# The router's transposes on VectorE in 32x32 blocks, with the blocks moved through DRAM

## The chip, the cores and the metric

The kernel runs on one core of one Trainium2 chip. The metric is the device time of one launch in microseconds (us), the median of the runs shown. Engines are called PE (TensorE), DVE (VectorE), ACT (ScalarE), POOL (GpSimd) and SP (SyncE, which here only issues DMAs).

## The reference

Three layers, in float32. First a two-way attention between 8x8 heads of 512 tokens (64 wide) and 32 states, which leaves 8 x 544 = 4352 tokens of 512 features. Then a gated layer on all of them, then a routed one:

```
x  = (silu(x @ w_gate) * (x @ w_val)) @ w_out          # 512 -> 1536 -> 512
do = x @ w_skip > 0                                     # tokens to compute
logits = x[do] @ w_route ; e = argmax(logits)           # 8 experts
out[do] = x + prob[e] * (relu(x @ w1[e]) @ w2[e])       # 512 -> 1024 -> 512
```

The change touches only how `x @ w_skip` and `x @ w_route` (nine scores a token) get their operand.

## The kernel before

The tokens go through the gated layer in nine blocks: eight blocks `b` of 512 attention tokens and a last block (`b == B`) of the 256 state tokens. A block takes 12 steps `f`, one for each 128 of the 1536 inner features. In a step PE runs `l1(b, f)` (gate and value: 24 matmuls with fp32 split into a high and a low half, all of them `L388`) and `l2` of the step before (12 matmuls, `L442` to `L444`). Between the two, ACT takes the tanh (`L395`), DVE makes `hv` (`L396`, `L399`), ACT casts the high half `hh` (`L407`), and POOL (in the last stretch DVE) subtracts the low half `hl` (`L408`). In the text a "step" is one such `(b, f)`. At the third and seventh step of a block `sw_two` also makes the next weights (`L171`, `L299`, `L300`), and the attention of the next block is spread over the same steps.

At a block's end `evac` copies four 128x512 results from PSUM into `x2` (two on ACT, `L457`, two on DVE, `L455`) and SP stores `x2` twice, to `out` and to `x2_dram` (`L463`). In the next block's steps the router works on it: `score_T` transposes each 128x512 quarter with four 128x128 PE transposes into one PSUM bank (`L479`) and DVE copies the bank into `x2T` (`L480`); `score_mm` multiplies `x2T` by the nine score columns `w9` (`L489`); ACT copies the result into a corner of `x2T` (`s9`, `L494`); `score_sum` transposes that back (`L500`, `L501`); `route_a` and `route_b` choose the expert and the slot, and POOL writes a record of each token into the table `tab` (`L565`, `L566`, `L575`). The token in partition `p` of quarter `j` is row `4p + j` of the block.

The table `sc_at` says at which steps these pieces stand in the program. From there a scheduler sets the order on each engine by its own estimate of times, and each engine runs its instructions in that order; SP too issues DMAs strictly in order, and a DMA that must wait for data holds up the ones behind it. Near the end of the eighth block `first_pick` and `first_load` choose one expert and SP loads its 4 MB of weights; the last block's scores are thus worked on beside the split of these weights (`L805`) and `first_xT` (`L824`), whose low halves go into the tile `fxl`. Two groups of `score_T` at the very end serve the last block itself. What follows after about 737 us (the experts) the change doesn't touch.

Of the kernel before, what the change touches and what calls it, by code (L numbers as in the profile page):

```python
# [7 lines left out]
F32 = mybir.dt.float32  # L8
F32R = mybir.dt.float32r
# [11 lines left out]
B, H, S, NS, D = 8, 8, 512, 32, 64  # L21
# [4 lines left out]
T = S + NS  # L26
# [6 lines left out]
SS = 32  # L33
# [18 lines left out]
def attention_then_two_moe_kernel(  # L52
# [13 lines left out]
    nc = tc.nc  # L66

    const = ctx.enter_context(tc.tile_pool(name="const", bufs=1, side="left"))
    dram = ctx.enter_context(tc.tile_pool(name="dram", bufs=1, space=bass.MemoryType.DRAM))
# [20 lines left out]
    with ExitStack() as ph:  # L90
        left = ph.enter_context(ExitStack())
        wts = left.enter_context(tc.tile_pool(name="wts", bufs=1, side="left"))
        ahl = left.enter_context(tc.tile_pool(name="ahl", bufs=2, side="left"))
# [13 lines left out]
        def side_bank():  # L107
            return ps_q.tile([128, 512], F32, name=ROLE[2], tag=ROLE[2])
# [5 lines left out]
        w9 = wts.tile([128, 4, SS], F32, name="w9")  # L114
# [235 lines left out]
        HT, HV = {}, {}  # L350
# [97 lines left out]
        def evac(b, half):  # L448
# [21 lines left out]
                        nc.sync.dma_start(out=dst, in_=x2[:, t])  # L470
            HV[b] = (x2, sml.tile([128, 4, 9], F32, name="sc"))

        def score_T(b, t):
            x2, sc = HV[b]
            if t == 0:
                late["x2T"] = late["p"].tile([128, 4, 512], F32, name="x2T")
            p = side_bank()
            for j in range(4):
                nc.tensor.transpose(p[:, 128 * j:128 * j + 128], x2[:, t, 128 * j:128 * j + 128], ident)  # L479
            nc.vector.tensor_copy(  # L480
                late["x2T"][:, :, 128 * t:128 * t + 128], p.rearrange("p (j c) -> p j c", j=4)
            )

        def score_mm(b):
            nt = 4 if b < B else 2
            p = side_bank()
            for j in range(4):
                for t in range(nt):
                    nc.tensor.matmul(  # L489
                        p[SS * t:SS * t + SS, :128], w9[:, j], late["x2T"][:, j, 128 * t:128 * t + 128],  # L490
                        start=(j == 0), stop=(j == 3),
                    )
            late["s9"] = late["x2T"][:, 0, :128]
            nc.scalar.copy(late["s9"][:SS * nt], p[:SS * nt, :128])  # L494

        def score_sum(b):
# [48 lines left out]
        def route_b(b):  # L545
            nt, comp, ex, oh, ohb, cum, t8, t1, bc, be = RT.pop(b)
            p = side_bank()
            rk = p[:, :nt * E].rearrange("p (a b) -> p a b", b=E)
            nc.tensor.matmul(rk, tri, ohb, start=True, stop=False)
            nc.tensor.matmul(rk, ones, cum, start=False, stop=True)  # L550
            sl = t8("sl")
            nc.vector.tensor_tensor(out=sl, in0=rk, in1=be(ecap), op=ALU.add)
            nc.vector.tensor_tensor(out=sl, in0=sl, in1=oh, op=ALU.mult)
            s1 = t1("slot")
            nc.vector.tensor_reduce(out=s1, in_=sl, op=ALU.add, axis=AX.X)
            nc.vector.tensor_scalar(comp, comp, -BIG, BIG, op0=ALU.mult, op1=ALU.add)
            si = t1("si", I32)
            nc.vector.tensor_tensor(out=si, in0=s1, in1=comp, op=ALU.add)
            g = t1("g")
            nc.vector.tensor_reduce(out=g, in_=ex, op=ALU.add, axis=AX.X)  # L560
            nc.vector.tensor_scalar(g, g, 1e-9, None, op0=ALU.add)
            rec = sml.tile([128, 4, 3], I32, name="rec")
            nc.vector.reciprocal(rec.bitcast(F32)[:, :nt, 1], g)
            if b < B:
                nc.gpsimd.iota(rec[:, :, 0], [[1, 4]], base=b * T, channel_multiplier=4)  # L565
                nc.gpsimd.iota(rec[:, :, 2], [[1, 4]], base=b * S, channel_multiplier=4)  # L566
            else:
                for q in range(4):
                    nc.gpsimd.iota(
                        rec[32 * q:32 * q + 32, :nt, 0], [[4 * T, nt]], base=q * T + S, channel_multiplier=1  # L570
                    )
                nc.gpsimd.iota(rec[:, :nt, 2], [[128, nt]], base=B * S, channel_multiplier=1)
            done = []
            for t in range(nt):
                d = nc.gpsimd.indirect_dma_start(  # L575
                    out=tab[:, :], out_offset=bass.IndirectOffsetOnAxis(ap=si[:, t:t + 1], axis=0),
                    in_=rec[:, t, :], in_offset=None, bounds_check=E * CAP - 1, oob_is_err=False,
                ).ins
                if not done:
                    after_tab(d)  # L580
                for o in done:
                    tc.declare_no_dep(d, o, reason="each token has a row of its own")
                done.append(d)
            TAB[:] = done
# [228 lines left out]
        def first_xT():  # L813
            B0["xh"] = [
                wts.tile([128, 2, 512], F32R, name="fxh", tag="srT"), ahl.tile([128, 2, 512], F32R, name="ah")
            ]
            B0["xl"] = [
                late["p"].tile([128, 2, 512], F32R, name="fxl"), ahl.tile([128, 2, 512], F32R, name="al")
            ]
            for t in range(NT1):  # L820
                p = pair_bank() if t == 2 else ps_x.tile([128, 512], F32, name=f"px{2 + t}")
                s = slice(128 * t, 128 * t + 128)
                for k in range(K1):
                    nc.tensor.transpose(p[:, 128 * k:128 * k + 128], B0["xr"][t][:, 128 * k:128 * k + 128], ident)  # L824
                for a in range(2):
                    split(
                        B0["xh"][a][:, :, s], B0["xl"][a][:, :, s],
                        p[:, 256 * a:256 * a + 256].rearrange("p (k c) -> p k c", k=2),
                    )
# [76 lines left out]
        with tc.manual_schedule(engines={getattr(mybir.EngineType, e) for e in ("Activation", "DVE", "Pool")}):  # L906
# [99 lines left out]

        steps = [(b, f) for b in range(B + 1) for f in range(NF)]
        sc_at = {
            False: ({3: 0, 4: 2, 5: 3}, {3: 1}, 7, 8, 9),
            True: ({1: 0, 2: 1, 3: 2, 4: 3}, {}, 5, 6, 8),  # L1010
        }
        for i, (b, f) in enumerate(steps):
            if i < HAND:
                continue
            if i > HAND:
                l1(b, f)
            nb, nf = steps[min(i + 2, len(steps) - 1)]
            if nb < B:
                if nb == 0 and nf % 2 and i > HAND:
                    sw(nb, (nf - 1) // 2)  # L1020
            elif i + 2 < len(steps):
                sw_tok(nf, 0)
                sw_tok(nf, 1)
            sb, sc = att_at.get(i, ([], []))
            if b:
                mid, end, mm, sm, rt = sc_at[b == B]
                if f in mid:
                    sb = [lambda: score_T(b - 1, mid[f])] + sb
                if f in end:
                    sc = sc + [lambda: score_T(b - 1, end[f])]  # L1030
                if f == mm:
                    sb = sb + [lambda: score_mm(b - 1)]
                if f == sm:
                    sb = sb + [lambda: score_sum(b - 1), lambda: route_a(b - 1)]
                if f == rt:
                    sb = sb + [lambda: route_b(b - 1)]
            if 0 < b < B and f in (2, 6):
                sb = [lambda: sw_two(b, f // 2 + 1)] + sb
            if b < B - 1 and f == 10:
                sb = [lambda: sw_two(b + 1, 0)] + sb  # L1040
            conv_step(1 if b == 0 and i > HAND else 0)
            wo_split(b, f)
            if b == 0:
                if i == HAND:
                    sb = [lambda: a_srT(0)] + sb
                if f == 7:
                    load_w9()
                if f == 4:
                    init_tab()
            if b == B - 1 and f == 10:  # L1050
                sr_split()
            if b == B - 1 and f == 11:
                first_pick()
                first_load()
            if b == B and f == 10:
                first_xT()
            pb, pf = steps[i - 1]
            l2(pb, pf, 0)
            if pf == NF - 1:
                if pb == 0:  # L1060
                    open_late()
                evac(pb, 0)
            for t in sb:
                t()
            conv_step(f % 2 if b == 0 else 0)
            l2(pb, pf, 1)
            if pf == NF - 1:
                evac(pb, 1)
            for t in sc:
                t()  # L1070
            for _ in range((f > 3) + 2 * (f > 9) if b == B else 0):
                todo.pop(0)(pin=tc.keep_in_program_order)
            if f == 8 and b + 2 < B:
                load_T(b + 2)
                load_x(b + 2)
# [492 lines left out]
```

## Time and profile before

| | |
|---|---|
| median of 3 runs | 1012.24 us (1008.66 to 1014.16) |
| profiled execution | 1007.3 us, span 1005.6 us, mean granted PE clock 0.977 |
| PE busy | 957.1 us (95%), 6502 matmuls |
| DVE busy | 567.7 us (56%) |
| ACT busy | 438.1 us (44%) |
| POOL busy | 419.1 us (42%) |
| DMA | 103.18 MB, mean 103 GB/s over the span |

The span runs from the first to the last instruction; the time adds what lies around it. Busy shares are averages over stages that have different limits, so the prediction reads the stage in which the changed instructions stand. PE's rows overlap, since matmuls are pipelined: the distance between two starts is what a matmul costs, not its own duration.

### The profile page before, as it was taken

The page shows a single profiled execution, that of the slowest core. Times are in us where ns is not written, and L with a number is a line of the kernel's source. Part 1 is how long each engine was busy: PE and PEld are TensorE (multiplying, and loading weights), DVE is VectorE, ACT ScalarE, POOL GpSimd, SP SyncE. Part 2 cuts the span into 40 slices and gives each one's busy share as a digit, 9 for nine tenths or more (in the row PEclk, how much of TensorE's full clock was granted, in tenths as well). Part 3 has the DMA queues.
Part 4 walks back from the last instruction along what each step waited for, and adds up shares of the span by engine and source line. Part 5 has one row for each costly group of instructions (what it writes and reads, how often), then busy time and mean ns, then how long its engine had stood idle before and what let it go on. Part 6 is the DMA issues. An engine that isn't in the chain of part 4 may idle for free. (4 is left out here: it accounts for less than half of the span.)

```text
span 1005.6 us, 16950 instructions
## 1 busy us (share of the span) xinstructions
PE 957.1 (95%) x6502; PEld 730.6 (73%) x6502; DVE 567.7 (56%) x1155; ACT 438.1 (44%) x792; POOL 419.1 (42%) x413
## 2 busy tenths in 40 slices
PE   3999999999999999999999999999998888989897
PEld 2555777777777777777777777789887666767786
DVE  6989565564564565556555544678763542552361
ACT  5876443444444354354353343446513441443240
POOL 2001343653553554544454353320246545645711
PEclk7999999999999999999999999999999899989899
DMA  9891401111031030130020020051126538634441
GB/s 357 295 331 47 165 5 46 73 54 46 6 121 45 1 126 7 41 126 3 2 84 1 2 84 1 1 207 78 29 78 226 175 133 270 212 99 157 159 160 53
DMA packets 38762, 103.18 MB, mean 103 GB/s; under 512 B 14661, under 2 KB 15949, under 8 KB 34696
## 3 DMA queue, kind: packets, MB, share of 16 engines
q1 hardware_dynamic: 27080, 88.06, 24.2%
q0 software_dynamic: 11584, 13.87, 4.4%
q8 instruction: 54, 0.88, 0.4%
q14 instruction: 44, 0.36, 0.1%
HBM read 99.93 MB, written 23.24 MB: 122 GB/s over the span
## 5 line engine op out<-in xcount | busy, mean ns | idle before, releaser
L408 POOL TENSOR_TENSOR hl<-hv,hh 128x512 fp32r<-128x512 f32 x82 | 106.4, 1298 | 191.7 <-ACT hh L407 191.7
L442 PE MATMUL px<-wh,hh 128*128 128x512 f32 x376 | 154.6, 411 | 0.2 <-ACT hh L407 0.2
L388 PE MATMUL q<-ah,sh 128*128 128x512 f32 (+1 forms) x368 | 139.9, 380 | 8.9 <-ACT ah L247 8.0
L443 PE MATMUL px<-wl,hh 128*128 128x512 f32 x376 | 148.0, 394 | 0.0
L444 PE MATMUL px<-wh,hl 128*128 128x512 f32 x376 | 147.9, 393 | 0.0
L421 POOL TENSOR_TENSOR wl<-wo,wh 128x512 fp32r<-128x512 f32 x82 | 105.9, 1292 | 94.2 <-ACT wh L420 94.1
L388 PE MATMUL q<-ah,sl 128*128 128x512 f32 (+1 forms) x368 | 135.8, 369 | 0.1
L388 PE MATMUL q<-al,sh 128*128 128x512 f32 (+1 forms) x368 | 134.8, 367 | 0.0
L396 DVE SCALAR_TENSOR_TENSOR t<-t,q 128x512 f32<-128x512 f32 (+1 forms) x100 | 65.3, 653 | 115.5 <-ACT t L395 115.1
L407 ACT CAST hh<-hv 128x512 fp32r<-128x512 f32 (+1 forms) x100 | 59.5, 595 | 130.3 <-DVE hv L399 129.6
L420 ACT CAST wh<-wo 128x512 fp32r<-128x512 f32 x100 | 61.9, 619 | 81.5 <-PE px L444 72.2
L442 PEld LDWEIGHTS px<-wh,hh 128*128 128x128 f32 x376 | 70.6, 188 | 34.3 <-issue 20.0
L388 PEld LDWEIGHTS q<-ah,sh 128*128 128x128 f32 x368 | 69.8, 190 | 29.6 <-ACT ah L247 8.5
L444 PEld LDWEIGHTS px<-wh,hl 128*128 128x128 f32 x376 | 70.6, 188 | 16.3 <-DVE hl L408 0.2
L395 ACT ACTIVATE t<-q 128x512 f32<-128x512 f32 (+1 forms) x100 | 57.1, 571 | 57.0 <-PE q L388 56.0
L443 PEld LDWEIGHTS px<-wl,hh 128*128 128x128 f32 x376 | 70.8, 188 | 12.8
L388 PEld LDWEIGHTS q<-ah,sl 128*128 128x128 f32 x368 | 69.8, 190 | 13.2 <-DVE sl L342 0.5
L388 PEld LDWEIGHTS q<-al,sh 128*128 128x128 f32 x368 | 69.7, 190 | 12.6 <-issue 1.0
L388 PE MATMUL q<-ah,fh 128*128 128x512 f32 x224 | 76.3, 401 | 0.0
L1316 DVE SCALAR_TENSOR_TENSOR hl<-p,hh 128x512 fp32r<-128x512 f32 x28 | 19.4, 691 | 94.8 <-ACT hh L1315 69.2
L399 DVE SCALAR_TENSOR_TENSOR hv<-t,q 128x512 f32<-128x512 f32 (+1 forms) x100 | 65.5, 655 | 11.0
L804 ACT CAST kwsb<-r 128x512 fp32r<-128x512 f32 x120 | 67.7, 625 | 6.3 <-PE p L1331 3.0
(292 smaller groups left out, 1911.7 us busy)
## 6 DMA issues: line engine op xcount, KB each, us to landing
s1w<-in_moe_w_dram SPq DMA_DIRECT2D x14, 1024.0 KB
s2w<-in_moe_w_dram SPq DMA_DIRECT2D x14, 1024.0 KB
raw<-in_w_in_dram SPq DMA_DIRECT2D x12, 1023.8 KB
xt<-in_x_dram SPq DMA_DIRECT2D x8, 1024.0 KB
out_dram<-x SPq DMA_DIRECT2D x8, 1024.0 KB
x_dram<-x SPq DMA_DIRECT2D x8, 1024.0 KB
xT<-in_xT_dram SPq DMA_DIRECT2D x7, 1024.0 KB
raw<-in_w_out_dram SPq DMA_DIRECT2D x6, 1023.8 KB
```

Source lines behind the costliest of these rows:

```text
L388: nc.tensor.matmul(p[:, :n], w, m, start=start, stop=stop)
L395: nc.scalar.activation(t[:, :n], pg[:, :n], AF.Tanh, scale=0.5)
L396: nc.vector.scalar_tensor_tensor(out=t[:, :n], in0=t[:, :n], scalar=1.0, in1=pg[:, :n], op0=ALU.add, op1=ALU.mult)
L399: nc.vector.scalar_tensor_tensor(out=hv[:, :n], in0=t[:, :n], scalar=0.5, in1=pv[:, :n], op0=ALU.mult, op1=ALU.mult)
L407: nc.scalar.copy(hh[:, :n], hv[:, :n])
L408: low_eng(b, f).tensor_tensor(out=hl[:, :n], in0=hv[:, :n], in1=hh[:, :n].bitcast(F32), op=ALU.subtract)
L420: pin(nc.scalar.copy(wh, w))
L421: pin(low_eng(b, f).tensor_tensor(out=wl, in0=w, in1=wh.bitcast(F32), op=ALU.subtract))
L442: nc.tensor.matmul(p, hh[:, s], wh, start=(f == 0), stop=False)
L443: nc.tensor.matmul(p, hh[:, s], wl, start=False, stop=False)
L444: nc.tensor.matmul(p, hl[:, s], wh, start=False, stop=(f == NF - 1))
L804: pin(nc.scalar.copy(hi, src))
```

## The change

For the eight blocks of attention tokens `score_T` is replaced by `score_pair(b, h)`, which takes two quarters at once (`h` is 0 or 1). DVE transposes each quarter in 32x32 blocks into `x2b`; four DMAs, one from each 32 partitions, write the blocks into a DRAM scratch `swap` with the block rows and columns exchanged; one DMA reads it back as half of `x2T`, whose layout is new. `score_mm` reads its 128 columns from there in four runs of 32. Tokens come out in another order, so the record's row numbers are made by eight small `iota`s in place of two. The last block keeps `score_T`. `x2b` has one buffer and shares it with `fxl`; `swap` has two.

```
+        def score_pair(b, h):
+            x2 = HV[b][0]
+            if h == 0:
+                late["x2T"] = late["p"].tile([128, 2, 4, 2, 4, 32], F32, name="x2T", tag="x2T")
+            x2b = late["p"].tile([128, 4, 2, 128], F32, name="x2b", tag="fxl")
+            swap = dram.tile([4, 32, 4, 256], F32, name="swap", bufs=2)
+            for t in range(2):
+                nc.vector.transpose(
+                    x2b[:, :, t].rearrange("p g (k q) -> p k g q", k=4),
+                    x2[:, 2 * h + t].rearrange("p (k g q) -> p k g q", k=4, g=4),
+                )
+            for a in range(4):
+                nc.sync.dma_start(
+                    out=swap[:, :, a].rearrange("g q x -> q g x"),
+                    in_=x2b[32 * a:32 * a + 32].rearrange("q g t x -> q g (t x)"),
+                )
+            nc.sync.dma_start(
+                out=late["x2T"][:, h].rearrange("p a t k q -> p (a t k q)"), in_=swap.rearrange("g q a x -> (g q) (a x)")
+            )
...
+            if b < B:
+                nt, of = 4, lambda j, t: x2T[:, :, t, :, j]
...
-                        p[SS * t:SS * t + SS, :128], w9[:, j], late["x2T"][:, j, 128 * t:128 * t + 128],
-                        start=(j == 0), stop=(j == 3),
+                        p[SS * t:SS * t + SS, :128], w9[:, j], of(j, t), start=(j == 0), stop=(j == 3),
...
-                nc.gpsimd.iota(rec[:, :, 0], [[1, 4]], base=b * T, channel_multiplier=4)
-                nc.gpsimd.iota(rec[:, :, 2], [[1, 4]], base=b * S, channel_multiplier=4)
+                for t in range(4):
+                    for k, o in ((0, b * T), (2, b * S)):
+                        nc.gpsimd.iota(
+                            rec[32 * t:32 * t + 32, :, k], [[128, 4]], base=o + t, channel_multiplier=4
+                        )
...
         sc_at = {
-            False: ({3: 0, 4: 2, 5: 3}, {3: 1}, 7, 8, 9),
-            True: ({1: 0, 2: 1, 3: 2, 4: 3}, {}, 5, 6, 8),
+            False: ({1: 0, 4: 1}, 7, 8, 9),
+            True: ({1: 0, 3: 1}, 6, 7, 8),
         }
```

The scheduler places the new instructions. On SP, after the second block (`x_1870` is its `x2`), the order before was:

```order
L463 DMA out_dram<-x_1870 128x2048
L463 DMA x_dram<-x_1870 128x2048
L160 DMA xT<-in_xT_dram 128x2048
L156 DMA zt<-in_zT_dram 128x128
L166 DMA xt<-in_x_dram 128x2048
```

and now it is (line numbers are those of the changed file):

```order
L485 DMA swap<-x2b 32x4x256
L463 DMA out_dram<-x_1870 128x2048
L463 DMA x_dram<-x_1870 128x2048
L485 DMA swap<-x2b 32x4x256 x3
L160 DMA xT<-in_xT_dram 128x2048
L489 DMA x2T<-swap 128x1024
L485 DMA swap<-x2b 32x4x256 x4
L489 DMA x2T<-swap 128x1024
L156 DMA zt<-in_zT_dram 128x128
L166 DMA xt<-in_x_dram 128x2048
```

One of the first pair's writes stands ahead of the two stores of 1 MB, three behind them; the read-back stands behind the load of 1 MB `xT`.

On DVE, in the third step of the following block (`sw_two`), before:

```order
L300 TENSOR_TENSOR fh<-q_1996,fh 128x512
L300 TENSOR_TENSOR fh<-q_1997,fh 128x512
L300 TENSOR_TENSOR sl<-q_1998,sh 128x512
L300 TENSOR_TENSOR sl<-q_1999,sh 128x512
L396 SCALAR_TENSOR_TENSOR t<-t,q_2035 128x512
L399 SCALAR_TENSOR_TENSOR hv<-t,q_2036 128x512
L480 COPY x2T<-q_2069 128x4x128
```

and now, where the first pair's two transposes stand at the end of the block before, around `L455`:

```order
L300 TENSOR_TENSOR fh<-q_2006,fh 128x512
L300 TENSOR_TENSOR fh<-q_2007,fh 128x512
L480 STREAM_TRANSPOSE x2b<-x_1870 128x4x4x32
L300 TENSOR_TENSOR sl<-q_2008,sh 128x512
L300 TENSOR_TENSOR sl<-q_2009,sh 128x512
L480 STREAM_TRANSPOSE x2b<-x_1870 128x4x4x32
L396 SCALAR_TENSOR_TENSOR t<-t,q_2045 128x512
L399 SCALAR_TENSOR_TENSOR hv<-t,q_2046 128x512
```

The second pair's transposes have moved into this step, ahead of the step's own `hv`, although the program asks for them only at the fifth.

On PE, the score matmuls of the eighth block stood between the two halves of `l2` in the last block's sixth step:

```order
L444 MATMUL px_6692<-wh,hl 128x512
L489 MATMUL q_6934<-x2T,w_114 32x128 x16
L442 MATMUL px_6703<-wh,hh 128x512
```

and now stand inside the tenth step's `l1` (bank `q_7181`), with the transpose of their result four matmuls behind them:

```order
L388 MATMUL q_7181<-ah,sh 128x256
L513 MATMUL q_6982<-x2T,w_114 32x128 x16
L388 MATMUL q_7181<-al,sh 128x256
L388 MATMUL q_7181<-ah,sl 128x256
L388 MATMUL q_7181<-ah,sh 128x256
L388 MATMUL q_7181<-al,sh 128x256
L523 MATMUL q_7054<-ident,x2T 128x128
```

The routing of the eighth block that hangs on them has moved back with them, into the last three steps before the experts.

## Rows read from the trace of the kernel before

**Rows 1.** Windows by stage: stretch, its us, busy us (x instructions), granted clock, DMA share, GB/s.

```profile
130.00:660.00 530.00, 530.00 (x3424) 398.83 (x3424) 292.67 (x611) 224.52 (x411) 255.37 (x222) 1.00 0.11 41
660.00:737.00 77.00, 76.75 (x549) 70.14 (x548) 60.78 (x184) 41.81 (x91) 10.91 (x16) 1.00 0.30 107
```

**Rows 2.** Timeline, PE, around one group of transposes: start us, us, engine, line, operation.

```profile
226.61 0.60 PE L479 MATMUL q<-ident,x 128*128 128x128 f32 x4
226.97 0.48 PE L442 MATMUL px<-wh,hh 128*128 128x512 f32 x1
227.28 0.39 PE L443 MATMUL px<-wl,hh 128*128 128x512 f32 x1
227.51 0.40 PE L444 MATMUL px<-wh,hl 128*128 128x512 f32 x1
```

**Rows 3.** Instructions of line 479: count, duration ns min/median/max, first and last start.

```profile
L479 PE MATMUL q<-ident,x x136: 270/272/328, 134.2 to 724.6; 128*128 128x128 f32 x136
```

**Rows 4.** Timeline, PE, the score matmuls of one block and what follows.

```profile
241.74 1.06 PE L489 MATMUL q<-x2T,w 128*32 128x128 f32 x32
242.72 0.50 PE L442 MATMUL px<-wh,hh 128*128 128x512 f32 x1
```

**Rows 5.** Groups by line: count | busy us, mean ns of one | idle before, releaser.

```profile
L480 DVE COPY x2T<-q 128x512 f32<-128x512 f32 x34 | 23.4, 689 | 24.8 <-PE q L479 24.8
...
L250 DVE TENSOR_TENSOR al<-aT,ah 128x512 fp32r<-128x512 f32 x16 | 19.1, 1196 | 16.4 <-ACT ah L247 16.4
...
L243 DVE STREAM_TRANSPOSE aT<-s 128x512 f32<-128x512 f32 x16 | 11.2, 699 | 0.2
...
L565 POOL IOTA rec<- 128x4 int32 x8 | 1.1, 134 | 0.1
```

**Rows 6.** Timeline, DVE, third step of a token block.

```profile
287.39 1.29 DVE L300 TENSOR_TENSOR fh<-q,fh 128x512 fp32r<-128x512 f32 x2 [2.02 <-ACT fh L299]
288.60 1.28 DVE L300 TENSOR_TENSOR sl<-q,sh 128x512 fp32r<-128x512 f32 x2
291.20 0.69 DVE L396 SCALAR_TENSOR_TENSOR t<-t,q 128x512 f32<-128x512 f32 x1 [1.32 <-ACT t L395]
```

**Rows 7.** Timeline, POOL, the low half that follows that step's hv.

```profile
293.50 1.29 POOL L408 TENSOR_TENSOR hl<-hv,hh 128x512 fp32r<-128x512 f32 x1 [2.29 <-ACT hh L407]
```

**Rows 8.** Timeline, PE, where that low half is first used.

```profile
298.69 0.40 PE L444 MATMUL px<-wh,hl 128*128 128x512 f32 x1
```

**Rows 9.** Timeline, SP's queue, one block's stores and the next load.

```profile
275.52 0.34 SPq L463 DMA_DIRECT2D out_dram<-x  x1
...
276.46 0.85 SPq L160 DMA_DIRECT2D xT<-in_xT_dram  x1
```

**Rows 10.** The page's part 3: packets, MB, their time as share of 16 engines' span.

```profile
q0 software_dynamic: 11584, 13.87, 4.4%
```

**Rows 11.** Windows of 1 us: the last with this block's DMA; the last with the expert load's.

```profile
284.00:285.00 1.00, 1.00 (x6) 0.82 (x5) 0.90 (x2) 0.00 (x0) 0.00 (x0) 1.00 0.65 270
683.00:684.00 1.00, 1.00 (x10) 1.00 (x10) 0.90 (x2) 0.36 (x1) 0.00 (x0) 1.00 0.20 82
```

**Rows 12.** Timeline, SP's queue, the first expert's loads and the last token block's stores.

```profile
662.88 0.42 SPq L769 DMA_DIRECT2D rec<-tab  x1
...
664.82 2.89 SPq L786 DMA_DIRECT2D r<-in_moe_w_dram  x5
...
669.00 1.02 SPq L463 DMA_DIRECT2D x_dram<-x  x1
```

**Rows 13.** Timeline, POOL, the gather that waits for the load of 662.88.

```profile
665.69 0.98 POOL L773 DMA_INDIRECT x0s<-x_dram,rec  x1 [7.50 <-DMA rec<-tab]
```

**Rows 14.** Timeline, DVE, last steps: the low half of the sixth.

```profile
692.09 0.42 DVE L408 TENSOR_TENSOR hl<-hv,hh 128x256 fp32r<-128x256 f32 x1
```

**Rows 15.** Timeline, PE, the tenth step of the last stretch begins.

```profile
704.39 0.28 PE L388 MATMUL q<-ah,sh 128*128 128x256 f32 x1
```

**Rows 16.** Windows, ten us of that stretch.

```profile
700.00:710.00 10.00, 10.00 (x74) 9.11 (x73) 9.97 (x35) 6.82 (x14) 0.75 (x1) 1.00 0.01 2
```

More of the change, by code (lines that the diff above doesn't have):

```diff
@@ L475, in score_T @@
             if t == 0:
-                late["x2T"] = late["p"].tile([128, 4, 512], F32, name="x2T")
+                late["x2T"] = late["p"].tile([128, 4, 512], F32, name="x2T", tag="x2T")
             p = side_bank()
@@ L484, in score_mm @@
         def score_mm(b):
-            nt = 4 if b < B else 2
             p = side_bank()
+            x2T = late["x2T"]
+            if b < B:
+                nt, of = 4, lambda j, t: x2T[:, :, t, :, j]
+            else:
+                nt, of = 2, lambda j, t: x2T[:, j, 128 * t:128 * t + 128]
             for j in range(4):
@@ L489, in score_mm @@
                     nc.tensor.matmul(
-                        p[SS * t:SS * t + SS, :128], w9[:, j], late["x2T"][:, j, 128 * t:128 * t + 128],
-                        start=(j == 0), stop=(j == 3),
+                        p[SS * t:SS * t + SS, :128], w9[:, j], of(j, t), start=(j == 0), stop=(j == 3),
                     )
-            late["s9"] = late["x2T"][:, 0, :128]
+            late["s9"] = x2T.rearrange("p h a t k q -> p (h a t k q)")[:, :128] if b < B else x2T[:, 0, :128]
             nc.scalar.copy(late["s9"][:SS * nt], p[:SS * nt, :128])
@@ L817, in first_xT @@
             B0["xl"] = [
-                late["p"].tile([128, 2, 512], F32R, name="fxl"), ahl.tile([128, 2, 512], F32R, name="al")
+                late["p"].tile([128, 2, 512], F32R, name="fxl", tag="fxl"), ahl.tile([128, 2, 512], F32R, name="al")
             ]
@@ L1025, in attention_then_two_moe_kernel @@
             if b:
[L1026 to L1030, printed above, removed]
+                pairs, mm, sm, rt = sc_at[b == B]
+                if f in pairs:
+                    sb = [lambda: score_pair(b - 1, pairs[f])] + sb
                 if f == mm:
```

## The prediction

> **What bounds the kernel now.** I read the windows by stage first, because a busy share over the span mixes stages. From 130 to 660 us, which is where the eight blocks run and where most of the router's transposes stand, PE is busy 530.00 of 530 us at the full granted clock, while DVE has 293, ACT 225 and POOL 255 us of work and the DMA engines are used 11% of the time [rows 1]. From 660 to 737 us, the last block, PE is still busy 76.75 of 77 us [rows 1]. So PE sets the pace where the change acts, and an instruction taken off PE there is worth its slot, as long as nothing else becomes late.
>
> **What is removed from PE.** The slot is read from starts, not from durations. A row of a 128x512 matmul starts 0.23 us after the one before (227.28 to 227.51). A group of four transposes starts at 226.61, the next matmul at 226.97 and the one after at 227.28 [rows 2]. Without the group that last one would have started 0.23 us after 226.61. The group therefore costs 227.28 - 226.61 - 0.23 = 0.44 us. Line 479 has 136 transposes [rows 3]; 8 of them serve the last block and stay, so 128 go, 32 groups, 4 in each block: 32 x 0.44 = 14.1 us. Of these, 7 x 4 x 0.44 = 12.3 us lie in steps up to about 660 us, and 1.8 us (the eighth block's) in the last stretch.
>
> [...]
>
> The score matmuls stay 16 a block, in 0.98 us (241.74 to 242.72) [rows 4]. Their operand now comes in runs of 32 columns. I take no change; the rivals have the other end.
>
> **What is added on DVE.** 32 copies of 0.689 us go, 22.0 us. 32 transposes of 128x512 come. Their nearest row is the attention's own 32x32 transpose from SBUF to SBUF, 0.699 us, so 22.4 us [rows 5]. Below I see nothing; above, the slowest 128x512 row of DVE in these blocks is the 1.196 us of the two-input subtraction [rows 5], which would make 16 us more, spread over eight blocks in which DVE is 55% busy. Its place matters more than its size. In the third step the four `L300` end at 289.88 and `L396` starts at 291.20, when ACT delivers [rows 6], so of 1.4 us of transposes 1.3 fit before it. Behind it, the step's low half is done at 293.50 + 1.29 = 294.79 us [rows 7] and PE needs it at 298.69 [rows 8]; two groups of transposes that stand between go, so 3.0 us of slack are left. I cost the transposes at nothing; that slack and the 1.3 us are their cover.
>
> **The new wait on DVE.** `x2b` has one buffer. The second pair's first transpose stands behind the two `fh`, at 288.6 us in these rows [rows 6], and waits until the first pair's four writes have landed; `hv` is queued behind it, and PE behind `hv`. In the rows SP issues the stores at 275.52 and `xT` at 276.46 [rows 9], and their 3 MB end in the window of 284 us, 65% full [rows 11]: 3.1 MB in some 9 us. The first write now stands ahead of the stores, three behind them, and `xT` behind those. The first pair's transposes sit among the copies of `evac`, which delays the stores by about 0.7 us. Two MB of stores then end near 282.5 us. The 0.52 MB of a pair go in packets of 1 KB; the nearest row is queue 0, whose 11584 packets of 1.2 KB on average took 4.4% of 16 engines' 1005.6 us, 708 us for 13.87 MB, or 313 GB/s over 16 engines [rows 10]: 1.7 us. A small load was issued by 663.30 and let its gather go at 665.69 [rows 12, 13], so landing takes up to 2.4 us. That gives 282.5 + 1.7 + 2.4 = 286.6 us, 2 us before DVE asks and 5 us before PE would notice.
>
> [...]
>
> Then the second pair's writes and its read-back have until the eighth step, some 30 us later; its traffic is 16.8 MB in a stage whose DMA engines are 89% idle. SP has nothing urgent behind these waits: the `zt` and `xt` it holds are issued for a block 80 us ahead. POOL gets six `iota`s of 0.134 us more a block [rows 5], 0.8 us on an engine with 275 of 530 us free. I cost all this at nothing.
>
> **The last stretch.** Here the first pair's writes queue behind 4 MB of expert weights, whose last loads SP issues from 664.82, and the stores up to 670 us [rows 12]. That traffic ends at about 683.2 us [rows 11]. So the pair lands near 683.2 + 1.7 + 2.4 = 687.3. The second pair's transposes now stand behind the sixth step's low half, which is at 692.09 [rows 14]; as four groups and the score matmuls (1.8 + 1.0 us) no longer stand ahead of it on PE, that is about 689.7, again in time. From there: 1.4 us of transposes, four issues of 0.34 us [rows 9], 1.7 us and 2.4 us give 696.6; the read-back, 1.7 + 2.4, gives 700.7. The score matmuls stand behind 16 of 24 matmuls (0.12 us each, half of 0.23) of the tenth step, which began at 704.39 [rows 15]: 704.39 + 1.9 - 2.8 = 703.5. The margin is 2.8 us. But the routing behind them now runs in the last three steps, where DVE has the weights to split and is already 9.97 of 10 us busy [rows 16], and PE waits for it twice (`L572`, `L573`) with only a step between. I set the loss at 1.8 us, just what the four groups saved; the bounds are a gain of 1.8 and a loss of 6, the routing's chain fully bare.
>
> **The sum.** -12.3 - 1.8 + 1.8 = -12.3 us. The profiled execution took 1007.3 us, so it would take 995.0. That execution is 0.5% under the median of the three runs, 1012.24; taken from the median, **999.9 us, say 1000**.
>
> **The rivals.**
>
> *The last stretch eats more.* If the queued writes or DVE's routing chain hold PE for 5 us net, the gain is 12.3 - 5 = 7 us: 1005. For it: 9.97 of 10 [rows 16]. Against: only a few us of slack are missing.
>
> *The new wait gives the gain back.* The pair lands not at 286.6 but beyond 288.6 + 3.0 = 291.6, and each us more stops PE in seven blocks. At 1.8 us more (293.4) the gain is gone: 1012. For it: the transfer has no row of its own and the queue is in order. Against: it needs 8.5 us for 0.52 MB in place of 1.7, 62 GB/s.
>
> *Slower.* The same wait decides for slower when it stops PE for (12.3 + 5) / 7 = 2.5 us a block, that is when the pair lands at 294.1, 9.2 us after the stores, so when its writes run below 57 GB/s. At 50 GB/s they take 10.5 us, the stop is 3.8 us a block, and 7 x 3.8 - 12.3 = +14: 1026. The score matmuls could do the same: if runs of 32 columns made their 0.98 us four times as long, 8 x 2.9 - 12.3 = +11, 1023. Against both: 313 GB/s for packets of this size, and nothing in the rows that slows PE by its operand's place.
>
> *The change does nothing* because PE would wait in the freed slots: against it speaks 530.00 of 530 us busy [rows 1].
>
> **How the numbers follow.** A measurement here can tell some 0.5%, 5 us, from no change. Forecast 0.64 (own bounds -9 to -14); last stretch 0.14, still a gain of over 5 us in most of it; gain given back or nothing 0.11; slower 0.11. So faster 0.64 + 0.10 = 0.74, within 5 us 0.04 + 0.11 = 0.15, slower 0.11. The full 14.1 us would give 998; the runs before scatter by some 3 us around their median, so the range begins at 995. To leave out no more than 2 in 10 it reaches to the case in which the gain is just given back, 1012; the forecast's own range, with the scatter, ends at 1006.
>
> **What would show it.** Right: PE again full up to about 650 us, two groups of PE transposes left, 32 transposes on DVE of 0.70 us each, and no DVE idle time of a microsecond that a DMA ends ahead of `x2b`. The score matmuls of a block still take 0.98 us. The last block's score matmuls start within a microsecond of their turn. Wrong: a row in which `x2b` waits on `swap`, PE waiting for `hh` or `hl` in a fourth step, or PE standing at `L572` and `L573` for more than 6 us together.

## The result, and the profile after

The changed kernel took 999.42 us, the median of 4 runs (996.60 to 1001.93); the kernel before, beside it, 1012.64 (1008.66 to 1014.16). The ratio is 0.9871 with a 95% interval of 0.9839 to 0.9903, so 10 to 16 us less. The prediction was 1000 us. The profiled execution took 1000.37 us, its span 998.6.

The windows by stage of the changed kernel, the columns as in [rows 1]:

```profile
130.00:650.00 520.00, 520.00 (x3346) 389.17 (x3345) 294.65 (x608) 227.04 (x417) 264.31 (x266) 1.00 0.21 71
650.00:727.00 77.00, 76.96 (x544) 70.91 (x544) 63.42 (x193) 42.56 (x91) 10.88 (x16) 1.00 0.40 134
```

PE is still full in both stages; what fell out of it made the stages shorter. DVE's work is what it was (22 us of copies out, 22 us of transposes in), and the DMA share went from 0.11 to 0.21 without PE noticing. The groups by line, DVE's and POOL's new work, and the transposes left on PE (instructions of line 499, the old 479):

```profile
L480 DVE STREAM_TRANSPOSE x2b<-x 128x512 f32<-128x512 f32 x32 | 22.2, 701 | 4.3 <-ACT x L457 4.0
...
L590 POOL IOTA rec<- 32x4 int32 x64 | 6.6, 127 | 1.2
```

```profile
L499 PE MATMUL q<-ident,x x8: 272/272/313, 713.3 to 715.2; 128*128 128x128 f32 x8
```

The spans say only roughly where the time went, because the start and the end of the program vary by several microseconds from run to run, together by 10 us between the two traces of the kernel before. Better is one instruction that both kernels have in the same place. Line 444, the last of the three products of `l2`, has 376 matmuls in either; their 25th stands in the third step of the second block, just ahead of the first transposes of a block result, their 343rd behind the seventh result's scores. Timeline, PE, these two rows of the kernel before:

```profile
133.31 0.40 PE L444 MATMUL px<-wh,hl 128*128 128x512 f32 x1
...
654.77 0.39 PE L444 MATMUL px<-wh,hl 128*128 128x512 f32 x1
```

and of the changed kernel:

```profile
138.06 0.39 PE L444 MATMUL px<-wh,hl 128*128 128x512 f32 x1
...
646.58 0.39 PE L444 MATMUL px<-wh,hl 128*128 128x512 f32 x1
```

654.77 - 133.31 = 521.46 us before, 508.52 after: 12.94 us less. With POOL's first gather of the experts' rows (742.55 before, 732.34 after) and the span's end this cuts the program into four stages, which serve all runs below:

| stage | before | after | difference |
|---|---|---|---|
| start, to the 25th matmul | 133.31 | 138.06 | +4.75 |
| blocks, 25th to 343rd | 521.46 | 508.52 | -12.94 |
| last stretch, 343rd to the first gather | 87.78 | 85.76 | -2.02 |
| end, first gather to the span's end | 263.05 | 266.26 | +3.21 |

Taken matmul by matmul, the difference between the two kernels is a staircase: flat for some 40 matmuls, then a fall of 1.36 to 1.39 us, then one of 0.47 to 0.50, and flat again, seven times. Three groups of transposes went at the first place, one at the second. In the last stretch it falls four times by 0.45.

### The profile page after: what moved, and what is told of

Read it like the earlier page. It is cut to its first block, busy times and chain, and to the rows that moved or that the text cites. A ratio compares the mean times of both kernels' runs of the same rounds, so it can differ in the third digit from the quotient of the medians.

```text
span 998.6 us, 16910 instructions
## 1 busy us (share of the span) xinstructions
PE 945.6 (95%) x6374; PEld 718.6 (72%) x6374; DVE 570.1 (57%) x1155; ACT 437.9 (44%) x792; POOL 428.9 (43%) x461
## 5 line engine op out<-in xcount | busy, mean ns | idle before, releaser
L442 PE MATMUL px<-wh,hh 128*128 128x512 f32 x376 | 151.9, 404 | 0.0
L396 DVE SCALAR_TENSOR_TENSOR t<-t,q 128x512 f32<-128x512 f32 (+1 forms) x100 | 65.4, 654 | 140.8 <-ACT t L395 140.2
L388 PEld LDWEIGHTS q<-ah,sl 128*128 128x128 f32 x368 | 69.8, 190 | 12.9 <-DVE sl L342 0.2
L388 PEld LDWEIGHTS q<-al,sh 128*128 128x128 f32 x368 | 69.8, 190 | 12.7 <-issue 1.2
L1339 ACT ACTIVATE hh<-p 128x512 fp32r<-128x512 f32 x28 | 16.7, 598 | 128.1 <-PE p L1337 63.3
```

The source lines that it names most:

```text
L388: nc.tensor.matmul(p[:, :n], w, m, start=start, stop=stop)
L396: nc.vector.scalar_tensor_tensor(out=t[:, :n], in0=t[:, :n], scalar=1.0, in1=pg[:, :n], op0=ALU.add, op1=ALU.mult)
L442: nc.tensor.matmul(p, hh[:, s], wh, start=(f == 0), stop=False)
```

## The experiments

The kernels of one batch ran on one chip, and different batches on different chips. The kernel before took 1013.70, 1015.26, 960.90 and 999.66 us beside the four batches, so whole times compare only inside a batch. All that follows is read from the stages.

**Both kernels again.** No edit.

> The kernel before, unchanged, for the scatter of each stage. The stages are cut at rows that both kernels have: the start (span start to the 25th of the 376 matmuls that multiply wh by hl), the blocks (25th to 343rd of them), the last stretch (343rd to the first gather of xr by POOL), the end (from there to the span's end). The first profile of before gave 133.31, 521.46, 87.78 and 263.05 us. Theory A (the change acts on PE's slots alone): blocks and last stretch come back within 0.2 and 0.5 us, while start and end scatter by some us of their own. Rival B (the change itself made the start 4.75 us and the end 3.2 us longer): start and end of before come back within 1 us too.

> The changed kernel, unchanged, for the scatter of each stage, cut as in the run before. The first profile of it gave 138.06, 508.52, 85.76 and 266.26 us. Theory A (only PE's slots changed): blocks within 0.2 us of 508.52, last stretch within 0.5 us of 85.76, start and end anywhere between those of the two kernels. Rival B (the change lengthens start and end): start near 138.1 and end near 266.3 again, within 1 us, while the second run of before stays near 133.3 and 263.1.

| run | start | blocks | last stretch | end | time |
|---|---|---|---|---|---|
| before_again | 135.84 | 521.65 | 87.94 | 270.57 | 1017.76 |
| after_again | 134.58 | 508.58 | 85.49 | 269.25 | 999.61 |

Theory A holds: blocks came back within 0.2 us and the last stretch within 0.3, while the start moved by +2.5 and -3.5 us and the end by +7.5 and +3.0. The +4.75 and +3.21 of the first table are scatter. What the change did is -13.0 in the blocks and -2.0 to -2.5 in the last stretch.

**The eighth result on PE again.**

```
                 pairs, mm, sm, rt = sc_at[b == B]
+                if b == B:
+                    pairs, mm, sm, rt = {1: 0, 2: 1, 3: 2, 4: 3}, 5, 6, 8
                 if f in pairs:
-                    sb = [lambda: score_pair(b - 1, pairs[f])] + sb
+                    go = score_pair if b < B else score_T
+                    sb = [lambda: go(b - 1, pairs[f])] + sb
```

The operand of `score_mm` and the `iota`s of this block are those of before.

> The changed kernel, but the eighth block's result, whose scores are made in the last stretch, is transposed on PE as before and at the places of before; the other seven blocks as changed. Theory A (the last stretch lost nothing, its four groups are pure gain): blocks as in the changed kernel, 508.5 us within 0.3, last stretch about 1.8 us longer than the changed kernel's, 87.6. Rival B, the sum of the prediction (the tight routing chain eats just what the four groups save): last stretch the same as the changed kernel's within 0.5 us, 85.8, or shorter. Rival C (the chain loses more than it saves, to be seen only later, when the experts begin): last stretch shorter by over 1 us.

Blocks 508.55, last stretch 88.73 us. Over the changed kernel's 85.49 in the same batch that is 3.2 us more, over the 87.94 of the kernel before 0.8 more. On PE's staircase the four groups cost 1.80 us (349th to 361st matmul), as theory A has it. Rival B, which was the prediction's sum, falls, and rival C with it: the last stretch lost nothing. At the last of these matmuls, the 376th, the difference is 1.75 us, so what goes beyond 1.8 us comes behind it. Its cause is open; the plan of this stretch is a new one in this kernel.

**The DVE work four times over.**

```
-            for t in range(2):
+            for t in [0, 1] * 4:
                 nc.vector.transpose(
```

> The changed kernel with each 32x32 transpose of the block result done four times over: 96 more of 0.70 us, 67 us of DVE work, 8.4 us in each block of 77.6 us. Theory A (DVE is off the path in the blocks and a planned order finds room for them): blocks within 1 us of 508.5; the last stretch, where DVE is full, longer by at most the 8.4 us of its own share. Rival B (slack of DVE is only the 1.3 + 3.0 us of the step named in the prediction, the rest goes to PE): 8.4 - 4.3 = 4.1 us a block, 508.5 + 29 = 537.

128 transposes ran instead of 32. Blocks 514.60 us, 6.1 more than the changed kernel, in five steps of 1.2 us, one in each of five blocks, where the weight load of `L171` on PE waits 1.1 us for line 396 on DVE; last stretch 86.58. For 59 us more of DVE work in the blocks PE lost 6, so A missed by 5 us, and B by 22. DVE's work is hidden nine tenths even at four times its size; at its real size nothing of it shows.

**More traffic ahead of the pair's writes, order free and order held.** All three add stores of the block result (1 MB each) ahead of the first pair's writes; in the last two an edge (a dependency that the planner must keep, without a semaphore on the chip) puts the second pair's transposes ahead of the step's `L396`.

```
+            for _ in range(4 * (1 - h)):
+                nc.sync.dma_start(out=dram.tile([128, 4, DM], F32, name="spare", bufs=2), in_=x2)
```

In held2 it is `2 * (1 - h)`. The held kernels also have

```
-            False: ({1: 0, 4: 1}, 7, 8, 9),
+            False: ({1: 0, 2: 1}, 7, 8, 9),
...
+                if 0 < b < B and f == 3:
+                    tc.add_manual_dep(lag.ins, late["tr"].ins.name, mybir.DependencyInfo(mybir.DependencyClass.NoSync, mybir.DependencyReason.DATA), reason="order")
```

where `lag` is line 396 and `late["tr"]` the last transpose; their lines from 397 on are numbered one higher.

> The changed kernel, and in each of the eight blocks four more stores of the block result (1 MB each) into an unused scratch, issued by SP right ahead of the first pair's four writes: 4.2 MB, some 10 us at the 420 GB/s that the stores reach. The first pair then lands some 10 us later than in the changed kernel (285.97 + 10 = 296 on its clock, where DVE came to the second pair at 289.7 and PE would have noticed from 292.7 on). The order of the work is planned anew, and the planner, which reckons with the transfer, now puts the second pair's transposes behind the next hv. Theory A (the wait costs only what stands behind it on DVE; where the planner knows of it, it moves the transposes away): blocks within 1 us of 508.5. Rival B (the landing is on PE's path whatever the order): 296 - 292.7 = 3.3 us a block in seven blocks, 508.5 + 23 = 532. Rival C (the added traffic itself hurts, through the next block's xT behind it or the memory's rate): slower by other amounts, with PE waiting on an xT row.

> The changed kernel with two more stores of 1 MB a block ahead of the first pair's writes, and with the order held: an edge without a semaphore keeps the second pair's transposes ahead of the next step's t and hv on DVE, where the changed kernel has them. 2.1 MB at 420 GB/s: the pair lands 5 us later, at 291.0 on the changed kernel's clock, 1.3 us after DVE asks (289.7). Theory A (the prediction's: 3.0 us of slack stand between DVE and PE): blocks 508.5 within 1 us. Rival B (no slack: each us of the wait stops PE): 7 x 1.3 = 9, 517.5.

> The changed kernel with four more stores of 1 MB a block ahead of the first pair's writes and the same held order. 4.2 MB at 420 GB/s: the pair lands at 296.0 on the changed kernel's clock, 6.3 us after DVE asks. Theory A (the prediction's slower rival: PE stops by what the landing lies beyond 292.7): 3.3 us a block in seven blocks, blocks 508.5 + 23 = 532, and the rows show x2b waiting on swap and PE waiting for hh or hl in that step. Rival B (DVE makes it up, PE never notices): 508.5. The run above with the same traffic and a free order tells the wait from the traffic.

| run | blocks | PE's waits for DVE in the blocks | last stretch |
|---|---|---|---|
| extra4 | 508.50 | none | 88.88 |
| held2 | 518.36 | 0.5 us, once | 89.22 |
| held4 | 536.63 | 10.0 us, 7 times, on line 300 | 88.92 |

extra4 is clear: 32 stores of 1 MB more cost the blocks nothing (the last stretch is 3 us longer), since the planner, which reckons with the transfer, puts the second pair's transposes behind `hv`. The held runs miss their theories and settle less than I meant them to. In held2 the planner put both of the second pair's transposes behind all four `L300`, so DVE came to `x2b` later than in the changed kernel: it waited there for the landing in five blocks, 1.0 us at most and 3.0 us together, and PE stood for 0.5 us in one of them, a step later. SP's read-back, which marks the landing, and DVE, in the fourth block, where there was no wait at all:

```profile
292.38 0.34 SPq L490 DMA_DIRECT2D x2T<-swap  x1
```

```profile
292.43 1.30 DVE L481 STREAM_TRANSPOSE x2b<-x 128x512 f32<-128x512 f32 x2
293.77 0.69 DVE L396 SCALAR_TENSOR_TENSOR t<-t,q 128x512 f32<-128x512 f32 x1
294.59 0.69 DVE L400 SCALAR_TENSOR_TENSOR hv<-t,q 128x512 f32<-128x512 f32 x1
```

This block runs 1.45 us behind the changed kernel, so `hv` stands at 293.14 on its clock, exactly where the changed kernel has it. The 9.8 us came 2.5 us later, where the planner had put PE's attention products in another order: a weight load of `L262` waits there 0.84 us for ACT's `eT`. So held2 does not test the 3.0 us of slack. In held4 the landing was at 302.58, 6.39 us behind: 296.2, as worked out (296.0); but the planner had also moved the attention's products that feed line 300, and DVE stood there, not at `x2b`. A late transfer that the planner knows of changes the order of four engines. To price the wait it must be one that the planner does not see.

**A transfer that is slow only on the chip.**

```
+            if h == 0:
+                spare = dram.tile([32, 128], F32, name="spare", bufs=2)
+                nc.sync.dma_start(out=spare.rearrange("c p -> p c"), in_=x2[:, 0, :32])
```

slow16 has 16 in place of 32. The blocks' order on PE, DVE, ACT and POOL is the changed kernel's.

> The changed kernel with one more DMA in each of the eight blocks, on SP ahead of the first pair's writes and of the stores: 128x32 numbers of the block result, written one by one, 4 bytes each, to places 512 bytes apart in an unused scratch (4096 packets, 16 KB). The planner takes it for short, so the order of the work on PE, DVE, ACT and POOL in the blocks is that of the changed kernel; only the queue is blocked for longer. No row has the price of a 4-byte packet; by queue 0 of the profile before (708 us of engine time for 11584 packets, 61 ns each) 4096 packets over 16 engines take 15.6 us, so the first pair would land at 285.97 + 15.6 = 301.6 on the changed kernel's clock. Theory A (the prediction's slower rival as priced: DVE waits at x2b, PE from 292.7 on): PE stops 301.6 - 292.7 = 8.9 us a block, or, whatever the packets cost, the landing less 292.7 us; the rows show x2b waiting on swap and PE waiting on hh or hl, seven times; blocks 508.5 + 62 = 571. Rival B (DVE and PE make the wait up elsewhere): blocks 508.5 within 2 us with x2b waiting all the same. Rival C (another wait on the blocked queue comes first, xT of the next block behind the writes): PE stops on an xT row instead.

Blocks 564.54 us: 8.0 a block. The waits, DVE and PE, of the whole run:

```profile
DVE x2b L480 <- DMA swap<-x2b: 66.1, 8, 8.9
```

```profile
PE q L388 <- DVE t L396: 40.3, 8, 6.0
```

The rival of the prediction is now there in full. In the fourth block (14.23 us behind the changed kernel) the read-back is issued at 312.90, on the changed kernel's clock at 298.67, and PE stops. No `xT` row holds PE, so rival C falls. Timeline, PE:

```profile
309.63 0.39 PE L444 MATMUL px<-wh,hl 128*128 128x512 f32 x1
316.07 0.79 PE L388 MATMUL q<-ah,fh 128*128 128x512 f32 x1 [6.05 <-DVE t L396]
316.66 0.63 PE L388 MATMUL q<-al,fh 128*128 128x512 f32 x1
```

The idle time is 6.05 us; the prediction's price, landing less 291.6 + 1.1 us on this clock, gives 5.97. But PE lost 8.36 us here on the staircase. The rest is in the clock. Windows of the same run:

```profile
308.00:310.00 2.00, 2.00 (x9) 1.31 (x7) 0.00 (x0) 0.00 (x0) 0.00 (x0) 1.00 0.99 410
310.00:316.00 6.00, 0.02 (x1) 0.00 (x0) 3.06 (x5) 0.00 (x0) 0.00 (x0) 0.81 0.83 319
316.00:318.00 2.00, 1.93 (x5) 1.55 (x6) 1.47 (x5) 0.72 (x2) 0.02 (x1) 0.50 0.79 190
318.00:320.00 2.00, 2.00 (x6) 1.59 (x5) 1.89 (x6) 0.42 (x1) 1.60 (x2) 0.50 0.29 82
320.00:322.00 2.00, 2.00 (x9) 1.56 (x8) 1.64 (x3) 0.52 (x1) 1.96 (x2) 0.85 0.67 225
```

After the stop PE was granted 0.50 until some time after 320: the twelve products of `fh` took from 316.07 to 321.02, 4.95 us, where the changed kernel takes 2.80. Those 2.15 us are a price of the stop that my rival did not have.

> The changed kernel with half the extra DMA of the run slow32: 128x16 numbers, 2048 packets of 4 bytes a block, same order of the work. There 4096 packets put the first pair's landing 12.7 us later (298.67 on the changed kernel's clock in the fourth block) and PE stood 6.05 us, 298.67 - 292.6, and lost 8.4 us with what followed at half the clock. Half the packets: landing 285.97 + 6.4 = 292.3, 2.6 us after DVE asks. Theory A (PE stops by what the landing lies beyond 292.6, and by nothing before): x2b waits some 2.6 us on swap, blocks 508.5 within 2 us. Rival B (what counts is the delay, without a threshold: 8.0 us a block for 12.7): 4.0 us a block, blocks 508.5 + 28 = 537.

Blocks 521.30 us, 12.8 more than the changed kernel, between the theories. Per block, from DVE's idle time before the second pair and the staircase at that place:

| block | 2 | 3 | 4 | 5 | 6 | 7 | 8 |
|---|---|---|---|---|---|---|---|
| DVE waits at x2b, us | 5.36 | 2.94 | 3.17 | 3.60 | 3.10 | 2.86 | 2.97 |
| PE loses, us | 2.92 | 0.33 | 0.57 | 1.02 | 0.50 | 0.26 | 0.36 |

In the last six columns the difference is always 2.6: DVE may wait 2.6 us for nothing, and every microsecond beyond that stops PE. So there is a threshold, against rival B, and it lies within 0.3 us of where A put it (292.6 less 289.7, or 2.9). What A left out: six of these blocks lose another 1.0 to 1.4 us one step later, where PE waits for line 396 again; DVE, having stood, comes to it late. That second bill makes 6.8 of the 12.8 us.

**The scratch laid out the other way.**

```
-            swap = dram.tile([4, 32, 4, 256], F32, name="swap", bufs=2)
+            swap = dram.tile([128, 4, 256], F32, name="swap", bufs=2)
...
-            for a in range(4):
+            nc.sync.dma_start(out=swap, in_=x2b.rearrange("p g t x -> p g (t x)"))
+            for g in range(4):
                 nc.sync.dma_start(
...
+                    out=late["x2T"][32 * g:32 * g + 32, h].rearrange("p a t k q -> p a (t k q)"),
+                    in_=swap[:, g].rearrange("(a q) x -> q a x", a=4),
                 )
```

> The changed kernel with the scratch laid out the other way: a pair leaves SBUF in one DMA from 128 partitions and comes back in four that each land on 32 partitions, instead of four out and one back. The changed kernel's second pair in the fourth block took 4.6 us from its first issue (292.23) to the issue of the read-back, which waits for the landing (296.86). Theory A (a DMA of 32 partitions is no slower than one of 128 for these packets; three issues and the fixed part of the landing are what counts): with three issues of 0.34 us less, 3.5 us from first issue to read-back, and PE's stages as in the changed kernel within 0.3 us, because the wait is off its path. [...]

Blocks 509.25 (+0.7), last stretch 84.30 (-1.2). SP's queue, fourth block:

```profile
273.21 0.33 SPq L484 DMA_DIRECT2D swap<-x2b  x1
273.82 0.34 SPq L463 DMA_DIRECT2D out_dram<-x  x1
274.22 0.61 SPq L463 DMA_DIRECT2D x_dram<-x  x1
275.92 3.91 SPq L486 DMA_DIRECT2D x2T<-swap  x4
280.21 0.34 SPq L484 DMA_DIRECT2D swap<-x2b  x1
```

The single write now stands ahead of the stores and has landed 2.71 us after its issue, where the changed kernel's second pair took 4.6 us from its first issue. The rate can be read from windows in which a pair's write has the DMA engines to itself. First the changed kernel's second pair in the fourth block, all of it and two parts of it, then the single write, before the stores behind it begin:

```profile
293.00:295.50 2.50, 2.50 (x13) 2.04 (x12) 2.29 (x6) 0.62 (x1) 0.89 (x1) 1.00 0.86 208
293.00:294.50 1.50, 1.50 (x9) 1.20 (x7) 1.33 (x5) 0.58 (x1) 0.00 (x0) 1.00 0.87 184
294.50:295.00 0.50, 0.50 (x4) 0.42 (x3) 0.47 (x2) 0.04 (x1) 0.39 (x1) 1.00 1.02 338
```

```profile
274.00:275.25 1.25, 1.25 (x7) 0.97 (x7) 1.25 (x3) 0.05 (x1) 0.63 (x1) 1.00 1.00 403
```

The 0.52 MB take about 2.5 us in four writes, at 208 GB/s, and 1.3 us in one, at 403 GB/s, so for the writes theory A falls: the four of 32 partitions ran at half the rate of the one of 128. The two forms also differ in the runs they write, 1 KB in the four and 4 KB in the one, so that the 32 partitions are the cause is not shown; but runs of 1 KB alone do not set the limit, since they went at 338 GB/s from 294.50 to 295.00. The reads were not compared. The 0.7 us in the blocks were more than the 0.3 expected; they come in steps of 0.13 to 0.17 us, one in each of six blocks, at the score matmuls. Their cause is open.

**The last block's own transposes by the same way.**

```
-        for t in range(2):
-            score_T(B, t)
-            todo.pop(0)()
+        score_pair(B, 0)
+        for t in range(2):
+            todo.pop(0)()
```

Here `x2b` is the unused half of `x2`, and `score_mm` and the `iota`s follow the new order of this block's tokens.

> The changed kernel, and the last block's result (256 tokens), which both kernels transpose on PE, now goes by DVE and the scratch too: two groups on PE fewer (0.9 us), one pair on DVE, four writes and one read-back more; the routing's row numbers follow the new order of tokens. Here no work of a next block hides the round trip: in the changed kernel the second pair of the last stretch took 3.8 us from its first write to the issue of its read-back and some 3 us to land, while the PE way takes 3.0 us from the first transpose (713.33) to the score matmuls (716.28). Theory A (on the path to the end the same change costs its latency): score matmuls some 6 us later, and the first gather with them, last stretch 85.6 + 6 - 0.9 = 90.7 us; blocks 508.5. Rival B (the first experts' matmuls fill the time and the routing chain has slack): last stretch 85.6 - 0.9 = 84.7.

Blocks 508.51, last stretch 97.18 us: 11.6 more than the changed kernel, where theory A had 6 - 0.9. Its queue and the score matmuls:

```profile
708.68 0.72 SPq L470 DMA_DIRECT2D out_dram<-x  x1
...
712.46 5.79 SPq L485 DMA_DIRECT2D swap<-x  x4
720.24 0.34 SPq L489 DMA_DIRECT2D x2T<-swap  x1
```

```profile
723.44 1.92 PE L513 MATMUL q<-x2T,w 128*32 128x128 f32 x16 [9.47 <-DMA x2T<-swap]
```

DVE had both transposes done by 710.7, but the writes stood behind the four stores of the same block until 712.46 and landed at 720.24, 7.8 us after their first issue. PE ran out of other work at 714.0 and stood for 9.47 us; then it was granted 0.50, so even the score matmuls took 1.92 us, where the changed kernel takes 1.07. The direction is A's; the queue ahead of the writes and the clock were missing from its price.

None of these versions beats the changed kernel in the stages that repeat: the 0.5 us that one_write gains there is little more than what two runs of one kernel differ by.

## Why the prediction was right, step by step

**PE sets the pace**: right, 520.00 of 520 us and 76.96 of 77.

**The groups' price**: 0.44 us was a little low. 28 groups in the blocks gave 12.94 us, 0.46 each; the four of the last stretch 1.79 us, 0.45 each. So the blocks gave 12.9 where the sum has 12.3.

**The score matmuls' operand**: right. 273 ns a row at the median as before, and the 16 of a block in 0.99 to 1.01 us in both kernels, in runs of 32 columns too.

**The transposes on DVE**: right, 0.70 us each (22.2 us for 32) against 0.699. PE was full in the blocks (520.00 of 520 us) and DVE 57% busy, and the blocks became 12.9 us shorter with the transposes on DVE.

**The wait at `x2b`**: right, and measured. The timeline of SP and DVE in the fourth block of the changed kernel:

```profile
276.47 0.33 SPq L485 DMA_DIRECT2D swap<-x2b  x1
277.10 0.34 SPq L463 DMA_DIRECT2D out_dram<-x  x1
277.49 0.44 SPq L463 DMA_DIRECT2D x_dram<-x  x1
277.98 3.53 SPq L485 DMA_DIRECT2D swap<-x2b  x3
281.61 1.36 SPq L160 DMA_DIRECT2D xT<-in_xT_dram  x1
285.97 0.34 SPq L489 DMA_DIRECT2D x2T<-swap  x1
```

```profile
288.51 1.29 DVE L300 TENSOR_TENSOR fh<-q,fh 128x512 fp32r<-128x512 f32 x2 [2.02 <-ACT fh L299]
289.71 0.70 DVE L480 STREAM_TRANSPOSE x2b<-x 128x512 f32<-128x512 f32 x1
290.34 1.25 DVE L300 TENSOR_TENSOR sl<-q,sh 128x512 fp32r<-128x512 f32 x2
291.51 0.69 DVE L480 STREAM_TRANSPOSE x2b<-x 128x512 f32<-128x512 f32 x1
292.31 0.69 DVE L396 SCALAR_TENSOR_TENSOR t<-t,q 128x512 f32<-128x512 f32 x1
```

This block stands 1.1 us later than in [rows 6]. Landing: 286.6 + 1.1 = 287.7 predicted, 285.97 here. DVE asks: 288.6 + 1.1 = 289.7 predicted, 289.71 here. `L396`: 291.20 + 1.1 = 292.3 predicted, 292.31 here, so the two transposes fit into the gap before it. The margin is 3.7 us where 2 were predicted. Two terms were off in opposite directions: the second pair, alone, moved in 2.5 us where the sum has 1.7, and from its last packets (by 295.50) to the issue of its read-back (296.86) went 1.4 us where the sum has 2.4 for the landing. The slack behind it came out as 2.6 us, predicted 3.0. One name was wrong: PE would not have stopped for `hh` or `hl` at line 442 or 444 but earlier, at line 388, whose bank `q` is read by line 396 first; both limits lie within half a microsecond here.

**The rivals on the wait**: their mechanism is real (slow32) and the threshold is right, but not their price: a stop of 6 us cost 8.4, because of the clock behind it (granted 0.50, 2.15 us lost), and in slow16 a stop of under 1 us brought another of 1.0 to 1.4 us.

**SP, POOL and the traffic at nothing**: right. The `iota`s took 0.127 us each, and even 4 MB more a block (extra4) did not move PE by 0.1 us in the blocks.

**The last stretch** is the step that failed. "I set the loss at 1.8 us, just what the four groups saved": no loss came, and the stretch is 2.0 to 2.5 us shorter. The score matmuls started at 694.89, 694.89 + 8.19 = 703.1 on the old clock, within half a microsecond of the predicted turn of 703.5, and PE waited for nothing from 650 to 727. From the 343rd matmul to the first gather PE has the same matmuls in both kernels, to within two, but for the 16 transposes (1.8 us); the kernel before also stood 0.2 us there for `hh`, and that makes the 2.0. The other pair of runs has 2.5, and what the 0.4 more are is open. I took 9.97 of 10 us busy [rows 16] for a chain without slack. Windows of the changed kernel, the same place and the ten microseconds behind it, into which most of the moved routing falls:

```profile
691.00:701.00 10.00, 10.00 (x97) 9.17 (x96) 8.36 (x27) 6.97 (x16) 0.00 (x0) 1.00 0.01 2
701.00:711.00 10.00, 10.00 (x69) 9.20 (x68) 9.82 (x34) 7.01 (x18) 3.25 (x3) 1.00 0.01 2
```

DVE is as full as before where the routing now runs, 9.82 of 10 us, and PE is full all the same. The share of a window says how much work an engine had, not which of it was urgent: the routing's instructions, under 0.2 us each, stand between the splits of the weights (6.5 of these 10 us), and PE's two matmuls for it (`L572`, `L573`) came without a wait.

**The sum**: 12.9 + 2.0 to 2.5 = 15 us by the stages, where 12.3 was forecast; by the medians 13.2, with the start and the end in it, which move by several microseconds from run to run. That the forecast came within 1 us of the measured median is in part this scatter; the stages show it 2.7 us short, 2.0 to 2.5 of them in the last stretch.

## What to carry to other kernels

When one engine is full, price the work that leaves it by the distance between starts, and look for the new path's cost only at the places where something waits on it: here one buffer, 3.7 us ahead of need, and 2.6 us of slack behind. The same change pays where the next block's work covers the round trip (0.46 us a group) and cost 11.6 us in the last block, where nothing does and the writes queue behind stores. To compare two kernels below a per cent, use the starts of an instruction that both have: they repeated within 0.2 us where the whole time moved by 4.

## What the runs showed of the hardware that I had not expected

A stop of several microseconds was dearer than its length. After 6.05 us without a matmul PE was granted 0.50 for the next 4 us or more and lost 2.15 us there; after the 9.47 us of last_pair it was at 0.50 from 723.4 to 734, with another stop of 1.9 us in between. The stops of 0.30 and 1.18 us in slow16 left it at 1.00.

4096 packets of 4 bytes delayed what stood behind them by 298.67 - 285.97 = 12.7 us: if 16 engines share them evenly, an estimate of 50 ns each, for 16 KB. In the same queue the traffic behind them ran at 410 GB/s (308 to 310 us in slow32).

The end of the program, which no change touched, took 263 to 274 us on some chips, 256 on another and 216 to 219 on a third. Its windows, first the changed kernel, then slow32 on that third chip, with the same work in it:

```profile
732.00:991.00 259.00, 232.18 (x1755) 187.45 (x1754) 106.24 (x175) 86.30 (x167) 132.67 (x132) 0.94 0.50 165
```

```profile
794.00:1002.00 208.00, 207.96 (x1752) 178.93 (x1751) 108.06 (x174) 88.39 (x167) 132.75 (x132) 1.00 0.59 206
```

There PE is full at the full clock; in the first it stands for 27 us in small pieces, with a granted clock of 0.94. 50 us between chips for the same program is four times what this change is worth. Why is open: nothing here varied that stage on purpose, and as each chip had one batch, chip and batch can't be told apart.
